# q for dK in an attention backward kernel: from a copy by tokens in DRAM to replicated copies on GpSimd and DMA transposes on chip

## The chip, the cores and the metric

The kernel runs on one core of a Trainium2 chip. The metric is the device time of one execution in microseconds (us). PE is TensorE, DVE VectorE, ACT ScalarE, POOL GpSimd, SP SyncE; SP does no arithmetic here and issues DMAs. POOL issues DMAs too, between its own operations. Each engine works through its instructions in program order.

## What is computed

The output and all gradients of two attention blocks whose outputs stand side by side. Block A is linear attention. Block B, which the change concerns, has 16 query heads and one shared key and value head (S = 2048 tokens, D = 448, head size 28). In short:

```python
q = (x @ wq).reshape(B, S, H, Dh).transpose(0, 2, 1, 3)
k = x @ wk
v = x @ wv
scores = einsum("bhqd,bkd->bhqk", q, k) * Dh ** -0.5
p = softmax(scores)
o = einsum("bhqk,bkd->bhqd", p, v)
b = o.transpose(0, 2, 1, 3).reshape(B, S, H * Dh) @ wo
out, vjp = jax.vjp(...); grads = vjp(grad_out)
```

The gradient of k is dK = sum over heads and queries of dS (keys by queries) times q. For it q must lie with the queries on the partitions, in the order that the transposed dS has.

## The kernel before

Work on block A and the projections of block B fill the first 218 us: `phase_A`, then `phase_B_pre`, which leaves q in SBUF as `R1` (`qT`, `qT_B`): per group g of four heads a tile of 128 partitions (four heads of 32 rows: a shift row, 28 rows of q, padding) by 2048 tokens.

Then comes the core loop (line 894), its order written out by hand under `tc.manual_schedule()`: the instructions of each engine run in the order in which the lines stand. It has `NU + 28` = 540 iterations u. The scores are cut into 64 blocks b of 8 iterations: a block is a chunk `qc` of 256 queries (8 of them) and a pair of heads (8 of them), an iteration is two key tiles of 128. What belongs to a block is spread over later iterations by fixed lags (`due(u, lag)`):

- iteration u computes scores on PE and their exp on ACT in two halves (lines 914 and 964, tile `eT`), and for iteration w = u-16 the product dS: its first half on DVE (line 925), its second by a copy on ACT (`cp`, line 927) and a product on POOL (line 928, tile `dsT`);
- DVE transposes dS in 32x32 blocks into `dsx` two iterations later (line 995);
- every fourth iteration (u%4 = 3) SP issues a DMA transpose of four iterations' `eT` into `eN` (line 966), read by `dv_mm` from u = 8b+20 on (line 978);
- the block's end takes POOL too: `o_norm` at u = 8b+10 makes `prod`, `don` and a copy (lines 808, 811, 812); `row_D` at u = 8b+12 reduces `prod` on DVE and finishes `don` on POOL (lines 816, 817); `don_T` on PE at u = 8b+14 transposes `don` (line 825), and the dS of block b needs the result from u = 8b+16 on;
- `dk_m` (line 834) multiplies `dsx` by `qX`, from u = 8b+27 on, two iterations at a time.

`qX[qc]` is q of one chunk with the queries on the partitions. The transposed dS has 32 queries in each of four partition groups a (for four groups of keys), so q stands there four times: `qX[qc]` is [128, 4, 2, 512], partition 32a+j holding tokens (b, j, s) of the chunk for every a. Before, it is made through DRAM:

- `phase_B_pre` transposes the first 1024 tokens by four DMA transposes into `qn` (line 598) and stores them in `qn_d` in DRAM (line 599), both on SP;
- the entry of the loop transposes the other 1024 into SBUF on SP (line 893), and POOL stores them at u = 34, 42, 50, 58 (line 930);
- four DMAs on POOL per chunk load 256 KB each from `qn_d`, one per partition group a (line 937): for chunk 0 at u = 10 to 22, chunk 1 at u = 66 to 78, and chunk qc from 2 on at u%64 = 34, 42, 50, 58 of the chunk before.

`qX` alternates between two pools of one buffer each. `wo` (line 940) is the output weight, loaded by POOL from DRAM at u = 86. `put_shift` (line 617) writes the shift rows of q by four small DMAs on POOL per 512 tokens; for the second half of the tokens it stands at u = 1.

## Time and profile before

| | |
|---|---|
| median of three runs | 1078.32 us (1070.82 to 1080.0) |
| the profiled execution | 1082.27 us, span of its instructions 1080.6 us |
| start of core loop (first exp) | 218.5 us |
| granted TensorE clock | 0.994 |
| busy: PE, DVE, ACT, POOL | 1026, 898, 873, 774 us |
| DMA packets of the queue of SP | 174 MB of 199 MB moved |
| qX loads (line 937) | 32 on POOL, issue 577 ns each, landing 3.5 to 13.2 us after issue |

The profile is one execution. Busy time is the time in which an engine had an instruction running. The chain follows the work that ended last back to what released it. A group's line has the engine and operation, tiles written and read, shapes, count, busy time and mean duration, then the idle time before it and what ended that idle time. Times in timelines are from the start of the span.

### The profile page before, as it was taken

To read this page: it belongs to the slowest core of one execution; us is meant where nothing else is said; L and a number is where in the kernel's file an instruction comes from. 1 tells how busy PE (TensorE), PEld (TensorE's weight loads), DVE (VectorE), ACT (ScalarE), POOL (GpSimd) and SP (SyncE) were. 2 spreads that over 40 slices of the span, in tenths; PEclk is the share of its full clock that TensorE was granted. 3 is DMA by queue.
4 is the path that set the end of the run, shared out by engine and by line. 5 is a ranking of instruction groups with operands and counts; after the bars stand their busy time and mean duration, and the time that the engine had idled before them with its cause. 6 is when DMAs were issued, how large, how long until landed. Compare 5 with 4: busy or idle time off the path is not lost.

```text
span 1080.6 us, 39970 instructions
## 1 busy us (share of the span) xinstructions
PE 1026.0 (95%) x16241; PEld 484.7 (45%) x16241; DVE 898.0 (83%) x1793; ACT 873.2 (81%) x1741; POOL 774.0 (72%) x1018
## 2 busy tenths in 40 slices
PE   9999999996999999999999999999999999999998
PEld 5555545432444444444444444444444444444434
DVE  7887400556999999999999999999999999999933
ACT  6463122585999999999999999999999999999622
POOL 6001242235899888888988988988988898888881
PEclk9999999997999999999999999999999999999999
DMA  9759899199999999999999999999999999999973
GB/s 265 160 110 199 173 204 228 30 185 151 204 208 211 203 202 188 200 180 210 179 185 197 196 195 187 203 181 188 185 209 187 196 198 162 206 187 181 223 133 90
DMA packets 668305, 199.34 MB, mean 184 GB/s; under 512 B 646056, under 2 KB 663760, under 8 KB 668120
## 3 DMA queue, kind: packets, MB, share of 16 engines
q1 hardware_dynamic: 655256, 174.18, 95.7%
q0 software_dynamic: 7904, 18.64, 6.8%
q10 hardware_dynamic: 4960, 3.96, 1.3%
q8 instruction: 127, 2.08, 0.8%
q14 instruction: 58, 0.48, 0.1%
HBM read 20.99 MB, written 12.94 MB: 31 GB/s over the span
## 4 chain that ended last, share of the span: by engine, by line
PE 37%; POOL 21%; ACT 18%; DVE 11%; issue 10%; DMA 4%; ACTq 0%; DVEq 0%; POOLq 0%
POOL dsT L928 16%; PE agen L82 14%; ACT cp L927 9%; ACT eT L964 7%; PE agen L661 7%; PE aacc L82 7%; PE aacc L661 6%; DVE dsx L995 4%; DVE dsT L925 2%; DMA eN<-eT 2%; POOL prod L808 2%; POOL don L811 1%; POOL R L812 1%; ACT eT L914 1%; DMA qX<-qn_d 1%
## 5 line engine op out<-in xcount | busy, mean ns | idle before, releaser
L928 POOL TENSOR_TENSOR dsT<-cp,eT 128x512 bf16<-128x512 bf16 x512 | 587.8, 1156 | 103.7 <-ACT cp L927 97.2
L995 DVE STREAM_TRANSPOSE dsx<-dsT 128x512 f32<-128x512 f32 x512 | 358.0, 699 | 2.8 <-POOL dsT L928 0.3
L925 DVE TENSOR_TENSOR dsT<-agen,eT 128x512 bf16<-128x512 f32 x512 | 342.1, 668 | 20.0 <-PE agen L661 15.2
L661 PEld LDWEIGHTS <-R 32*128 32x128 bf16 (+1 forms) x9104 | 225.3, 94 | 276.1 <-issue 239.5
L914 ACT ACTIVATE eT<-aacc 128x512 bf16<-128x512 f32 x512 | 313.2, 612 | 26.7 <-PE agen L661 15.8
L927 ACT ACTIVATE cp<-agen 128x512 bf16<-128x512 f32 x512 | 315.4, 616 | 12.3 <-PE agen L661 11.2
L964 ACT ACTIVATE eT<-aacc 128x512 bf16<-128x512 f32 x512 | 321.7, 628 | 0.0
L661 PE MATMUL agen<-dsx,qX 32*32 32x512 bf16 x4096 | 269.0, 376 | 3.5 <-DMA qX<-qn_d 3.5
L661 PE MATMUL agen<-doT,R 32*128 32x256 bf16 x2048 | 248.1, 270 | 3.3 <-DVE dsT L925 1.6
L661 PE MATMUL aacc<-R,R 32*128 32x256 bf16 (+1 forms) x2240 | 218.8, 269 | 5.8 <-DVE oTs L804 1.3
L661 PE MATMUL agen<-eT,R 128*32 128x256 bf16 x2048 | 158.2, 275 | 0.1
L661 PE MATMUL agen<-dsT,R 128*32 128x256 bf16 x2048 | 157.3, 275 | 0.1
L661 PEld LDWEIGHTS <-qX 32*32 32x32 bf16 x4096 | 80.1, 89 | 118.4 <-issue 54.6
L661 PE MATMUL aacc<-eN,don 128*32 128x512 bf16 x1024 | 98.1, 383 | 4.3 <-DMA eN<-eT 4.3
L82 PEld LDWEIGHTS <-R 128*128 128x128 bf16 (+1 forms) x517 | 41.0, 99 | 43.9 <-issue 12.3
L407 POOL COPY pk<-R 128x256 bf16<-128x256 bf16 x4 | 1.6, 397 | 73.8 <-DVE R L367 73.7
L82 PE MATMUL agen<-R,R 128*128 128x448 bf16 (+1 forms) x180 | 42.9, 366 | 0.5 <-ACT R L226 0.5
L661 PEld LDWEIGHTS <-don 128*32 128x32 bf16 x1024 | 33.9, 98 | 5.3 <-issue 4.7
L423 DVE TENSOR_TENSOR osb<-aacc,pr 64x448 bf16<-64x448 f32 x2 | 1.2, 617 | 39.1 <-DMA out_dram<-osb 24.9
L825 PE MATMUL aacc<-identB,don 128*32 128x128 bf16 x256 | 18.6, 224 | 14.0 <-POOL don L817 10.2
L949 DVE TENSOR_SCALAR R<-agen 64x256 bf16<-64x256 f32 x64 | 27.3, 427 | 3.6 <-PE agen L661 1.6
L517 ACT ACTIVATE wdq<-agen 128x448 bf16<-128x448 f32 x16 | 8.7, 543 | 24.7 <-PE agen L82 24.7
(232 smaller groups left out, 987.7 us busy)
## 6 DMA issues: line engine op xcount, KB each, us to landing
qX<-qn_d POOLq DMA_DIRECT2D x32, 256.0 KB, 4.4
out_dram<-osb ACTq DMA_DIRECT2D x22, 112.0 KB
eN<-eT SPq DMA_TRANSPOSE x128
xa<-in_A_x_dram SPq DMA_DIRECT2D x8, 224.0 KB
ga<-in_grad_out_dram SPq DMA_DIRECT2D x4, 448.0 KB
xa<-in_grad_out_dram POOLq DMA_DIRECT2D x4, 448.0 KB, 5.8
out_dram<-wdq POOLq DMA_DIRECT2D x8, 224.0 KB, 4.9
eT<-in_grad_out_dram SPq DMA_DIRECT2D x4, 448.0 KB
```

Of the source, the lines that this page charges most:

```text
L82: nc.tensor.matmul(out_ap, lhsT=lhsT, rhs=rhs, start=start, stop=stop, tile_position=(0, 0))
L661: nc.tensor.matmul(out, lhsT=lhsT, rhs=rhs, start=start, stop=stop, tile_position=pos, skip_group_check=True)
L808: nc.gpsimd.tensor_tensor(out=prod[b][:], in0=dnv, in1=os_, op=ALU.mult)
L811: nc.gpsimd.tensor_tensor(out=dn[:], in0=dnv, in1=r_[:].to_broadcast([P, 2, 2, 32]), op=ALU.mult)
L825: nc.tensor.transpose(tp2[q:q + 32, qb * P:(qb + 1) * P], don[b][:, qb, h, :], identB[:, :], tile_position=(0, q))
L914: nc.scalar.activation(out=eT(u)[:, 0, :], in_=sp[0][:, :], func=ACT.Exp, scale=scale)
L925: nc.vector.tensor_tensor(out=dst[:, 0, :], in0=dp[0][:, :], in1=ew[:, 0, :], op=ALU.mult)
L927: nc.scalar.activation(out=cp[:, :], in_=dp[1][:, :], func=ACT.Copy)
L928: nc.gpsimd.tensor_tensor(out=dst[:, 1, :], in0=cp[:, :], in1=ew[:, 1, :], op=ALU.mult)
L949: nc.vector.tensor_scalar(out=qT_B[g][64 * hp:64 * hp + 64, qc * 256:(qc + 1) * 256], in0=oq[64:128, 0:256], scalar1=scale, scalar2=None, ...
L964: nc.scalar.activation(out=eT(u)[:, 1, :], in_=sp[1][:, :], func=ACT.Exp, scale=scale)
L995: nc.vector.transpose(out=dsx[b][:, tp, :, :, :].rearrange("p h t c -> p (h t c)").bitcast(F32), in_=dsT[y][:, :, :].rearrange("p h c -> p ...
```

## The change

`qn`, `qn_d` and all that reads or writes them go. In the loop, POOL copies q of one chunk and one group of four heads from `R1` into a new tile `qst` (one buffer), four times side by side, in two instructions (one for each s) in two successive iterations; then SP issues one DMA transpose of `qst` (128x1024) into the columns of group g of `qX[qc]`. For chunk 0 this happens at u = 0 to 7, two iterations per group, the transpose in the second; for chunk qc+1 at u%64 = 32 to 63 of chunk qc, eight iterations per group: copies at u%8 = 0 and 1, after that iteration's product on POOL, the transpose at u%8 = 3, on SP behind that iteration's transpose of `eT`. The load of `wo` moves from u = 86 to the entry of the loop. `qX[0]` and the even chunks move to the other of the two pools.

```diff
-            if qc == 1:
-                for g in range(4):
-                    nc.sync.dma_start_transpose(qn[:, :, g * P:(g + 1) * P], qT[:, g, 0:1024])
-                nc.sync.dma_start(qn_d[0:1024, :].rearrange("(t p) c -> p t c", p=P), qn)
...
+        qst = pp_.tile([P, 8, 4, 32], BF16, name="qst", bufs=1)
...
+        def qc_copy(qc, g, s):
+            src = qT_B[g][:, qc * 256:(qc + 1) * 256].rearrange("p (b j s) -> p b j s", b=4, s=2)[:, :, :, s]
+            nc.gpsimd.tensor_copy(out=qst[:, :, :, :].rearrange("p (b s) a j -> p b s a j", s=2)[:, :, s, :, :],
+                                  in_=src.unsqueeze(2).to_broadcast([P, 4, 4, 32]))
...
-            qn = pqa_.tile([P, 8, 512], BF16, name="qX")
-            for g in range(4):
-                nc.sync.dma_start_transpose(qn[:, :, g * P:(g + 1) * P], R1[:, g, 1024:2048])
+            nc.gpsimd.dma_start(wo, wo_d[:, 0:D].rearrange("(g p) c -> p g c", p=P))
+            qc_T = None
...
-                for n in {34: (0,), 42: (1,), 50: (2,), 58: (3,)}.get(u, ()):
-                    nc.gpsimd.dma_start(qn_d[1024 + 256 * n:1280 + 256 * n, :].rearrange("(t p) c -> p t c", p=P),
-                                        qn[:, 2 * n:2 * n + 2, :])
-                for a in {10: (0,), 14: (2,), 18: (1,), 22: (3,), 66: (0,), 70: (2,), 74: (1,), 78: (3,)}.get(u, ()) or {
-                        34: (0,), 42: (2,), 50: (1,), 58: (3,)}.get(u % 64, ()) * (96 < u < 448):
-                    qc = u // 64 + (u > 96)
-                    if a == 0:
-                        qX[qc] = (pqa_ if qc % 2 else pqb_).tile([P, 4, 2, 512], BF16, name="qX")
-                    nc.gpsimd.dma_start(qX[qc][32 * a:32 * a + 32, :, :, :].rearrange("j b s c -> j b (s c)"),
-                                        qn_d[qc * 256:(qc + 1) * 256, :].rearrange("(b j s) c -> j b (s c)", b=4, s=2))
-                if u == 86:
-                    nc.gpsimd.dma_start(wo, wo_d[:, 0:D].rearrange("(g p) c -> p g c", p=P))
+                if u < 8 or 32 <= u % 64 and u < 448:
+                    qc, (g, i) = (0, divmod(u, 2)) if u < 8 else (u // 64 + 1, divmod(u % 64 - 32, 8))
+                    if i == 0 and g == 0:
+                        qX[qc] = (pqb_ if qc % 2 else pqa_).tile([P, 4, 2, 512], BF16, name="qX")
+                    if i < 2:
+                        qc_copy(qc, g, i)
+                    if i == (1 if u < 8 else 3):
+                        qc_T = (qc, g)
...
+                    if qc_T:
+                        qc, g = qc_T
+                        nc.sync.dma_start_transpose(
+                            qX[qc].rearrange("p b s c -> p (b s) c")[:, :, g * P:(g + 1) * P], qst[:, :, :, :].rearrange("p n a j -> p (n a j)"))
+                        qc_T = None
```

The last lines stand behind the transpose of `eT` (line 966) and, like it, under `if hasS`.

## The prediction

> **What bounds the kernel now.** I read the page first (parts 1, 4, 5), then the chain in order of time and the waits for the first 60 us of the core loop, then the timeline of POOL for one group of eight iterations, then the DMA transposes on SP by tile, source line and timeline.

> ```profile
> PE 1026.0 (95%) x16241; PEld 484.7 (45%) x16241; DVE 898.0 (83%) x1793; ACT 873.2 (81%) x1741; POOL 774.0 (72%) x1018
> POOL dsT L928 16%; PE agen L82 14%; ACT cp L927 9%; ACT eT L964 7%; PE agen L661 7%; PE aacc L82 7%; PE aacc L661 6%; DVE dsx L995 4%; DVE dsT L925 2%; DMA eN<-eT 2%; POOL prod L808 2%; POOL don L811 1%; POOL R L812 1%; ACT eT L914 1%; DMA qX<-qn_d 1%
> L928 POOL TENSOR_TENSOR dsT<-cp,eT 128x512 bf16<-128x512 bf16 x512 | 587.8, 1156 | 103.7 <-ACT cp L927 97.2
> L407 POOL COPY pk<-R 128x256 bf16<-128x256 bf16 x4 | 1.6, 397 | 73.8 <-DVE R L367 73.7
> ```

> The core loop is 540 iterations u. The start times of L914 in the trace put u=0 at 218.5 us and u=511 at 1003.6 us, about 1.5 us each. In the stretch 500 to 600 us ACT is busy 99%, DVE 98%, PE 96%, POOL 89%: no engine has room, and POOL's L928 is the longest entry of the chain although POOL idles 104 us before it.

> Start of the loop, chain in order of time and waits:

> ```profile
> 232.62 16.89 DMA eN<-eT
> 255.79 10.60 DMA qX<-qn_d
> ```

> ```profile
> PE aacc L661 <- DMA eN<-eT: 4.3, 1, 4.3
> PEld L661 <- DMA qX<-qn_d: 3.8, 1, 3.8
> ```

> Two transfers are late there: the second eN transpose, then the fourth qX load. Iterations 16 to 23 take 19.1 us and 24 to 31 take 18.8 us, where 40 to 63 take 12.3 us per eight.

> Steady state, POOL's timeline (start, duration; last column the idle time before):

> ```profile
> 595.23 1.15 POOL L928 TENSOR_TENSOR dsT<-cp,eT 128x512 bf16<-128x512 bf16 x1 [0.32 <-ACT cp L927]
> 596.33 0.57 POOL L937 DMA_DIRECT2D qX<-qn_d  x1
> 596.91 0.44 POOL L808 TENSOR_TENSOR prod<-R,oTs 128x128 f32<-128x128 bf16 x1
> 597.30 0.41 POOL L811 TENSOR_TENSOR don<-R,rl 128x128 bf16<-128x128 bf16 x1
> 597.77 0.29 POOL L812 CAST R<-oTs 128x128 bf16<-128x128 f32 x1
> 598.02 2.26 POOL L928 TENSOR_TENSOR dsT<-cp,eT 128x512 bf16<-128x512 bf16 x2
> 600.25 0.21 POOL L817 TENSOR_TENSOR don<-Dq,rl 128x4 bf16<-128x4 f32 x1
> ```

> At u%8=2 POOL falls 1.3 us behind and has caught up by u%8=7. With a qX load in the group, eight iterations take 12.16 us; without, 12.0. The 0.15 us sits at u%8=6, where PE waits for don (L817). So POOL has no slack left in a group with a load: whatever it loses at u%8=0 to 4 comes out again as a wait of PE at u%8=6.

> SP, by tile, source line and timeline (durations ns min/median/max in the first two):

> ```profile
> L966 SPq DMA_TRANSPOSE eN<-eT x128: 4760/5421/12268, 226.6 to 1005.2; - x128
> ```

> ```profile
> L598 SPq DMA_TRANSPOSE gaT<-R x4: 1243/1269/1386, 212.4 to 216.7; - x4
> ```

> ```profile
> 1011.01 1.28 SPq L955 DMA_TRANSPOSE R<-R  x1
> ```

> An eN transpose holds SP 5.25 us from the end of its exp in a group without a load, 5.8 us with one, out of 6.05 us per four iterations. L598 and this L955 have the new transpose's size (128x1024). By the semaphore updates in the trace, L598 landed 3.4 us after it began, on idle DMA engines; the L955, issued behind an eN, 4.7 us after.

> [...] while qX loads run, eN goes from 5.25 to 5.8 us, and to 9 and 12 us at 232 and 241 us. [...] The trace has 2.0 to 3.4 us from the end of a 128x1024 transpose on SP to its last update. [...] here all are on SP, so the new ones queue with eN. [...] copies of 256 and 448 elements take 397 and 561 ns, 0.85 ns each.

> **The change, step by step**, against the profiled execution's span of 1080.6 us (1082.3 us by its own clock; the median of the runs shown is 1078.3, so I carry differences over to that).

> Removed. (a) The congestion at the start: 19.1+18.8 us for u=16 to 31. From the undisturbed even and odd iterations around them (1.45 odd, 1.8 even while do_proj runs, 1.5 later) I make it 13.0+12.3, so -12.5. (b) The last qX load (u=442) landed 13.2 us after issue; its eN held SP 8.5 us and the group took 13.5 us, not 12.15: -1.4. (c) The loads of u=66 to 78: 12.17, 12.15 against 12.0: -0.3. The four stores L930 and nine transposes and one store on SP before the loop (212 to 227 us) go too; u=0 does not wait for them, since PE's sel matmuls end at 217.9 and its first score matmuls follow at once. Their worth is in (a).

> Copies for loads in steady state. Two copies of 512 elements: 0.185+512x0.00085=0.62 us each, about 0.58 back to back, against one load issue of 0.58 in the same group. Copies stand at u%8=0 and 1. POOL's lag in a group, from L928 at 1.13 back to back and iterations of 1.48, 1.45, 1.68, 1.45: +0.25, +0.55, then the three of L808 to L812 to 1.2 at u%8=3 (now 1.27), and L817 starts with 0.88 (now 0.91). Net 0. Bounds for the copy, whose source steps two elements and repeats four times: 0.55 to 0.8 us, as no copy here has that pattern; each 0.1 us costs 0.2 per group, so -2 to +11 over 28 groups. I take 0.

> The new wait. qst is one buffer. Copies of group g+1 (u%8=0) wait until the transpose of group g has landed, and that one is issued at u%8=3 behind the eN of the same iteration. From the end of that exp: eN 5.25, gap 0.1, new transpose 1.3, landing 2 to 3.4 later, I take 2.9 (between L598's 2.0 and the L955's 3.4): 9.5 us. POOL reaches the copy when L928 of u%8=0 ends, 8.26 us after the same exp (mean of the second halves). So POOL stands about 1.25 us. Behind the copy on POOL are L928, L808 to L812, L817; for these wait the DVE transposes (L995), row_D and don_T, so PE loses it at u%8=6. That slip moves the next copy too, so the next group waits little: of four groups the first copy is free, the second and fourth wait. 2x1.2x7=17 us. Bounds: landing 2.0 gives about 5, 3.9 gives 27. SP itself: 5.25+1.4+5.25+0.2=12.1 per group of 12.16, just enough.

> The start. POOL now: wo load issue to 219.0, first copy to 220, put_shift (8x0.56) to 224.5; the second copy waits for these to land (they share POOL's queue with wo's 448 KB), about 226.2. Transpose 0 is issued at 226.9 and lands at 230.3; copies 1 to 231.5; transpose 1 stands behind eN(3) (228.1 to 233.2), lands 237.8; copies 2 to 239, transpose 2 lands 242.5; copies 3 to 243.7. Only then L808 of block 0, which ran at 233.6. DVE waits in row_D(0), PE in don_T(0): +9.8, with PE idle. eN and qX are then in time (eN(7) lands about 248.5, needed about 252.7). Bounds: 5 to 13. Moving wo costs its 0.8 us there, counted.

> Sum: -12.5-1.4-0.3+9.8+17=+12.6, a span of 1093 and a run of **1091 us**. Own range of this case 1084 to 1099.

> **Rivals.** (1) The landing is early enough (8.3 us or less after the exp): POOL doesn't stand, the start gives +9.8 against -14.2: -4, 1074 (to 1078 with small waits). For it: SP lands some small transposes 1.1 us after their end early in the trace. Against: those were alone. Chance 0.22. (2) The other side, faster: the round trips at the start don't hold POOL. If copies 3 are done before L808 of block 0 is due (233.6), all -14.2 stays; with early landings as in (1), 1064. It decides from 4 us per round trip less than I have; eN(3) in between speaks against it. Chance 0.08. (3) Landing at 3.9 us or copies at 0.8 us: +24 to +32 in all, 1102 to 1110. Both in part give the same. Chance 0.18. The transposes might also make dv_mm late: its slack is 13 iterations (19 us) against about 9; left out.

> **How the numbers follow.** Main case 0.52. The bound of 1% (about what can be told from no change) is 1067.5 and 1089.1. Faster: rival 2, 0.08. Within: rival 1 and the lower third of the main case, 0.39. Slower: the rest, 0.53. The range 1070 to 1112 leaves out rival 2 and the far end of 3.

> **What would show it.** In the new profile: waits of POOL's qst copy on DMA qX<-qst, about 1.2 us each and some 14 to 21 of them in the loop; a chain with DMA qX<-qst in it; at the start one long wait of PE or DVE for POOL prod or don near 235 to 245 us and no wait for eN; PE's waits at L825 for POOL don grown from the 32 us of now; copies near 0.6 us; eN back to about 5.3 us everywhere. If the copies wait for nothing, my landing time is wrong; if PE still waits for eN or qX, the start is.

## The result, and the profile after

The changed kernel takes **1110.99 us** (median of four runs, 1110.52 to 1113.82), against 1079.16 us for the kernel before beside it: ratio 1.0318, 95% interval 1.0264 to 1.0373. The forecast was 1091 us. The measured time has the forecast's sign and lies inside its range, but the loss, 32 us, is two and a half times the 12.6 us of the sum. The profiled execution ran 1110.71 us with a span of 1109.0 us; the granted TensorE clock is 0.98, where it was 0.994.

The page of the changed kernel, parts 1, 2, 4 and 5 (PEld is TensorE's weight load; a group's line: busy us and mean ns, then the idle time before it):

```profile
PE 1038.0 (94%) x16241; PEld 488.2 (44%) x16241; DVE 898.7 (81%) x1793; ACT 874.3 (79%) x1741; POOL 788.0 (71%) x1046
...
PEclk9999999988999999999999999999999999999999
...
POOL dsT L928 16%; PE agen L81 14%; ACT cp L927 11%; ACT eT L960 8%; PE agen L656 8%; PE aacc L656 7%; PE aacc L81 6%; DMA qX<-qst 2%; POOL qst L832 2%; DVE dsx L996 2%; DVE dsT L925 1%; ACT eT L914 1%; PE aacc L821 1%; POOL prod L804 1%; POOL don L807 1%
...
L928 POOL TENSOR_TENSOR dsT<-cp,eT 128x512 bf16<-128x512 bf16 x512 | 588.3, 1156 | 92.5 <-ACT cp L927 86.0
...
L832 POOL COPY qst<-R 128x512 bf16<-128x512 bf16 x64 | 38.9, 611 | 35.8 <-DMA qX<-qst 29.1
```

DVE and ACT do the work they did, to about 1 us, and no share says what was lost. What is new is a group that stands before it works: the 64 copies are busy 38.9 us and POOL is idle 35.8 us ahead of them, 29.1 us of that for the landing of a transpose. PE is busy 12 us *longer* for the same 16241 matmuls: they ran slower. Who waits, over the whole span (total us, times, longest):

```profile
PEld L821 <- POOL don L813: 40.3, 44, 10.9
...
POOL qst L832 <- DMA qX<-qst: 29.1, 16, 5.1
...
PE aacc L821 <- POOL don L813: 26.3, 16, 10.6
...
DVE Dq L812 <- POOL prod L804: 16.9, 10, 11.7
```

PE now waits 66.6 us for `don` in `don_T` (L821); before (there L825) it was 32.0 us:

```profile
PEld L825 <- POOL don L817: 21.8, 45, 1.5
...
PE aacc L825 <- POOL don L817: 10.2, 29, 1.2
```

By the start times of L914, u=511 begins 29.3 us later than before. 1.5 us of that is the entry of the loop, 220.0 against 218.5 us; the kernels below enter at 218.0 to 220.2 us whatever is changed in them, so this isn't the change's. (Each of the seven traces that enter at 220.0 us or later has 3.4 us at a granted clock of 0.50 at 51 us, and none of the other seven has.) The first 32 iterations take 59.1 us (57.3 before). In the windows of 64 iterations the second halves, u%64 = 32 to 63, of the first seven, where the copies stand, take 26.5 us more; all the rest of the loop takes 0.6 us less.

One such stand, that is, a time in which POOL has work and waits, on the timeline of POOL (start, duration; in brackets the idle time before):

```profile
596.71 0.61 POOL L832 COPY qst<-R 128x512 bf16<-128x512 bf16 x1 [1.32 <-DMA qX<-qst]
597.26 0.58 POOL L729 DMA_DIRECT2D out_dram<-R  x1
597.87 1.17 POOL L928 TENSOR_TENSOR dsT<-cp,eT 128x512 bf16<-128x512 bf16 x1
...
603.96 0.21 POOL L813 TENSOR_TENSOR don<-Dq,rl 128x4 bf16<-128x4 f32 x1
```

The copy of u%8=0 waits 1.32 us. Seven microseconds on, `don` is finished that much later (L813), and PE, which has stood in `don_T` for it, goes on. What that does to PE shows in the same stretch cut into four windows of 3.4 us (window, its length, then busy us and count by engine, PEclk, DMA share, GB/s):

```profile
597.60:601.00 3.40, 3.22 (x64) 1.37 (x64) 2.63 (x5) 3.16 (x7) 3.38 (x5) 1.00 1.16 207
601.00:604.40 3.40, 1.72 (x34) 0.59 (x30) 2.77 (x5) 2.91 (x6) 3.34 (x7) 1.00 1.17 113
604.40:607.80 3.40, 3.40 (x48) 1.13 (x38) 2.32 (x4) 1.61 (x4) 2.29 (x3) 0.50 1.49 277
607.80:611.20 3.40, 3.16 (x76) 1.46 (x72) 2.75 (x6) 2.89 (x7) 2.47 (x3) 0.99 0.92 133
```

In the second window PE is busy half the time. In the third the granted clock is 0.50 ("half clock" below), and PE, busy without a pause, gets through 48 matmuls where the window behind it has 76. The group of eight iterations takes 15.35 us in place of 12.0: 1.3 us of standing, half a microsecond for the store of an output tile that POOL issues in this group (L729), and 1.5 us of slow clock. The stand was in the prediction; the clock was not.

### The profile page after: what moved, and what is told of

Its sections match the earlier page's. It is cut to its first block, busy times and chain, and to the rows that moved or that the text cites. A ratio compares the mean times of both kernels' runs of the same rounds, so it can differ in the third digit from the quotient of the medians.

```text
span 1109.0 us, 40031 instructions
## 1 busy us (share of the span) xinstructions
PE 1038.0 (94%) x16241; PEld 488.2 (44%) x16241; DVE 898.7 (81%) x1793; ACT 874.3 (79%) x1741; POOL 788.0 (71%) x1046
## 4 chain that ended last, share of the span: by engine, by line
PE 38%; POOL 21%; ACT 21%; issue 11%; DVE 5%; DMA 3%; ACTq 0%; SPq 0%; POOLq 0%; DVEq 0%
POOL dsT L928 16%; PE agen L81 14%; ACT cp L927 11%; ACT eT L960 8%; PE agen L656 8%; PE aacc L656 7%; PE aacc L81 6%; DMA qX<-qst 2%; POOL qst L832 2%; DVE dsx L996 2%; DVE dsT L925 1%; ACT eT L914 1%; PE aacc L821 1%; POOL prod L804 1%; POOL don L807 1%
## 5 line engine op out<-in xcount | busy, mean ns | idle before, releaser
L928 POOL TENSOR_TENSOR dsT<-cp,eT 128x512 bf16<-128x512 bf16 x512 | 588.3, 1156 | 92.5 <-ACT cp L927 86.0
L925 DVE TENSOR_TENSOR dsT<-agen,eT 128x512 bf16<-128x512 f32 x512 | 342.0, 668 | 19.7 <-PE agen L656 14.7
L914 ACT ACTIVATE eT<-aacc 128x512 bf16<-128x512 f32 x512 | 312.9, 611 | 53.2 <-PE agen L656 26.2
L927 ACT ACTIVATE cp<-agen 128x512 bf16<-128x512 f32 x512 | 314.7, 615 | 12.3 <-PE agen L656 11.2
L656 PE MATMUL agen<-dsx,qX 32*32 32x512 bf16 x4096 | 272.5, 381 | 0.0
L656 PE MATMUL aacc<-R,R 32*128 32x256 bf16 (+1 forms) x2240 | 222.9, 271 | 6.5 <-DVE oTs L800 1.1
L656 PE MATMUL agen<-eT,R 128*32 128x256 bf16 x2048 | 160.5, 278 | 0.1
L832 POOL COPY qst<-R 128x512 bf16<-128x512 bf16 x64 | 38.9, 611 | 35.8 <-DMA qX<-qst 29.1
L81 PEld LDWEIGHTS <-R 128*128 128x128 bf16 (+1 forms) x517 | 41.2, 99 | 44.6 <-issue 13.3
L821 PE MATMUL aacc<-identB,don 128*32 128x128 bf16 x256 | 18.8, 225 | 33.6 <-POOL don L813 26.3
L656 PEld LDWEIGHTS <-don 128*32 128x32 bf16 x1024 | 34.5, 98 | 0.6
L821 PEld LDWEIGHTS <-don 128*32 128x32 bf16 x256 | 11.0, 94 | 47.9 <-POOL don L813 40.3
```

The source lines that it names most:

```text
L81: nc.tensor.matmul(out_ap, lhsT=lhsT, rhs=rhs, start=start, stop=stop, tile_position=(0, 0))
L656: nc.tensor.matmul(out, lhsT=lhsT, rhs=rhs, start=start, stop=stop, tile_position=pos, skip_group_check=True)
L821: nc.tensor.transpose(tp2[q:q + 32, qb * P:(qb + 1) * P], don[b][:, qb, h, :], identB[:, :], tile_position=(0, q))
L832: nc.gpsimd.tensor_copy(out=qst[:, :, :, :].rearrange("p (b s) a j -> p b s a j", s=2)[:, :, s, :, :], in_=src.unsqueeze(2).to_broadcast([ ...
L914: nc.scalar.activation(out=eT(u)[:, 0, :], in_=sp[0][:, :], func=ACT.Exp, scale=scale)
L925: nc.vector.tensor_tensor(out=dst[:, 0, :], in0=dp[0][:, :], in1=ew[:, 0, :], op=ALU.mult)
```

## Experiments

**Theory.** The loop loses by the meeting of the copy at u%8=0 with the landing of a transpose that was queued behind eN on SP. Each stand of POOL costs its own length, and in seven of the 14 cases a stretch of half clock on PE besides. **Rivals:** the copies' time on POOL; the 32 more transposes on SP and the DMA engines, making eN late; at the start, DMA traffic in place of the chain on POOL.

**1. The transpose at u%8=2.** One digit of the changed kernel is changed:

```diff
-                    if i == (1 if u < 8 else 3):
+                    if i == (1 if u < 8 else 2):
```

> The loop's q transposes are issued at u%8=2 instead of 3, so they stand in SyncE's order with no eN transpose directly ahead of them; one staging tile, copies and number of DMAs as in the changed kernel. Theory (the copy of the next group waits for the landing of a transpose that was queued behind eN, and each such stand of GpSimd idles TensorE): the transpose lands about 4 us after u%8=2, long before u%8=0, GpSimd's wait on it in the loop falls from about 25 us to under 2, each second half of a window comes back to 97-98 us per 64 iterations, time 1111 - 26 = 1085 (1081-1089). Rival (the 64 DMAs more on the same queue and DMA engines make eN or other loads late): no change, 1107-1112. Rival (the GpSimd time of the copies itself): no change, 1107-1112.

Measured: **1079.69 us**, ratio to the kernel before 0.9998 (0.9969 to 1.0027). The second halves take 48.0 to 48.6 us where they took 50.7 to 54.5, 30.1 us less in all. Waits in the loop, 262 to 1000 us, of which none is for qst:

```profile
PEld L821 <- POOL don L813: 16.7, 42, 1.1
PE aacc L821 <- POOL don L813: 4.9, 14, 0.8
```

The same copies, the same 32 transposes (64 is the number of the copies), one buffer: both rivals for the loop fall. The 30.1 us are above the 26 expected because copies in place of loads turned out better than even, see below; the start, which was not changed, was 3.4 us shorter in this execution besides (see "The start").

**2. The copies alone**, in the kernel before, where nothing reads what they write:

```diff
+                if 32 <= u % 64 and u < 448 and u % 8 < 2:
+                    qc_copy(u // 64 + 1, (u % 64 - 32) // 8, u % 8)
```

> The kernel before with the loop's 56 copies added on GpSimd at their places; nothing reads the tile they write, and q still comes by DRAM. Theory (waits, not work): GpSimd has the time, 1079 within 4 us. Rival (the 0.6 us copies delay GpSimd's dsT products, and TensorE with them): the second halves grow by 3 to 4 us each, 1100-1106.

Measured: **1092.57 us**, 1.0104 (1.008 to 1.0128), between the two ranges expected. Groups take 12.55 us where the kernel before has 12.16 and experiment 1 has 12.0: a load issue (0.58 us) in a group costs 0.15 us, two copies (1.2 us) cost nothing, all three 0.55 us. So the two copies use up what POOL can take ahead of `don`; the changed kernel stands right at that limit. That fits with every stand of POOL coming out whole at PE.

**3. The start alone.** Chunk 0's copies go into four tiles of the dsT pool:

```diff
+                    if u < 8 and i == 0:
+                        qstart[g] = pd_.tile([P, 2, 512], BF16, name="dsT").rearrange(
+                            "p h (n a j) -> p (h n) a j", a=4, j=32)
```

> Chunk 0 alone: its four copies go into four tiles that are free then (of the dsT pool), so no copy at u<8 waits for a transpose; the loop keeps its one tile and its late transposes. Theory (the start loses its gain to the chain copy-transpose-copy on GpSimd, which makes prod and don of block 0 late at u=14): u 0-31 falls from 59.1 us to 48-50 us, time 1111 - 10 = 1101 (1098-1104). Rival (the first blocks are slow for another reason, DMA traffic of the output weight and the q rows at entry): u 0-31 stays at 57-60, time 1108-1112.

Measured: **1104.04 us**, 1.0216 (1.0161 to 1.0272). u=0 to 31 takes 49.15 us, not 59.13; u=14 takes 1.16 us, not 12.20. The start is as the theory says. The total gives back 7 us and not 10, just outside the range expected: from u=32 to 511 this execution took 2.9 us more than that of the changed kernel.

**4. Both edits**, those of 1 and 3.

> Both edits: transposes at u%8=2 and own tiles for chunk 0. Theory: the two add, 1111 - 26 - 10 = 1075 (1070-1080), a little faster than the kernel before. Rivals as with each alone: 1085 if the start has another cause, 1101 if the loop has.

Measured: **1070.85 us**, 0.991 (0.9878 to 0.9941). They add. At u=20 there was a new stop; waits between 240 and 256 us:

```profile
DVE dsT L930 <- DMA qX<-dsT: 2.6, 1, 2.6
```

The dsT product of u=20 got the tile that the fourth transpose of chunk 0 was still reading: borrowed storage, the same kind of wait at another place. So the copies of chunk 0 moved into a `dsx` buffer, which is needed from u=26 on:

```diff
+        stage0 = px_.tile([P, 8, 2, 2, 256], BF16, name="dsx").rearrange(
+            "p (g n) h t c -> p g (n h t c)", g=4)[:, :, 0:1024].rearrange("p g (n a j) -> p g n a j", a=4, j=32)
```

> Transposes at u%8=2, and chunk 0's four copies into four parts of a dsx buffer (first needed at u=26) instead of dsT tiles (needed again from u=16). Theory (in the earlier form VectorE's dsT product of u=20 waited for a transpose that still read its tile): the stop at u=20 and its slow iterations go, u 0-31 falls from 50.1 to 45-46 us, time 1071 - 4.5 = 1066 (1062-1070). Rival (u=20 stands for something else): 1069-1073.

Measured: **1069.66 us**, 0.9897 (0.9854 to 0.9939). u=0 to 31 takes 45.80 us, with no stop. The total lies in both ranges expected; it is the stop that went which decides. Of the 4.3 us gained there, the profiled execution gave 3.0 back in one group at u=56 to 63, where a copy still waited 1.64 us for a transpose and half clock followed. That transpose belongs to u=50, and SP began it at u=55:

```profile
300.05 1.26 SPq L972 DMA_TRANSPOSE qX<-qst  x1
```

It landed 3.5 us after its end, within the 1.3 to 3.9 us of the others; what was late is SP. With the transposes of chunk 0 in its queue it falls 10 us behind at the start, and in the first window its eN still begin 4 to 7 us after their exp. The q transposes of that window start 6.1 to 7.1 us after the exp of their iteration, those of the other windows 0.4 to 4.8 us. So even at u%8=2 there is little room while SP is behind.

**5. A stand without a DMA.** In that kernel, idle copies of growing size on POOL stand in for the wait:

```diff
+                    if qc and i == 0 and g % 2:
+                        qf = qst[:, :, :, :].rearrange("p n a j -> p (n a j)")
+                        for n in [1024] * (qc // 4) + [256 * (qc % 4)] * (qc % 4 > 0):
+                            nc.gpsimd.tensor_copy(out=qf[:, 0:n], in_=R1[:, 0, 0:n])
```

> A GpSimd copy that does no work for the result is put ahead of the q copies at u%64=40 and 56, of 256, 512, 768, 1024, 1280, 1536 and 1792 elements in windows 1 to 7 (about 0.3 to 2.1 us); transposes at u%8=2 and own tiles for chunk 0, so GpSimd never waits for a transpose in the loop. It stands in for the wait. Theory (TensorE is idle as long as GpSimd is late[...]): groups of eight iterations take 12.0 us plus the copy up to about 1.1-1.2 us, and from 1.3 us on 12.0 plus the copy plus 1.5 to 2 us, with 2 to 3 us of granted clock near 0.6 behind don_T. Rival (the low clock has to do with the transposes or the DMA wait, not with the idle): 12.0 plus the copy at every size, clock 1.0.

Measured in one execution: **1091.62 us**. Without an idle copy the two groups take 12.55 (12.0 in windows 1 and 2) and 12.0 us; the first also issues the store of an output tile on POOL. A star marks a group with a stretch of half clock:

```
window                 1      2      3      4      5      6      7
idle copy, us       0.40   0.61   0.82   1.04   1.44   1.64   1.87
group of u%64=40   13.79  12.67  14.62* 15.04* 14.12  16.20* 14.54
group of u%64=56   12.44  12.67  12.88  13.09  14.86* 13.76  15.40*
```

(13.79 holds a real wait of 1.3 us for a transpose as well; it is the only one of this loop.) Without a star a group takes its base plus the copy, to 0.13 us; with one, 1.25 to 1.53 us more, and 2.0 us in column 6, where the half clock lasted two windows of the raster below. So the half clock needs no DMA wait, and the rival falls. But the step that I expected, between 1.2 and 1.3 us, is wrong too: 0.82 us brought a stretch and 1.64 us did not. In the traces of the kernels before and changed every change of the clock lies on one raster of 3.413 us (the stretches of half clock from 232 to 990 us are 3.413, 6.827 and 17.067 us long), so I took PE's busy share in the raster window just ahead (busy with the profile's modelled ends). In these two traces, from 232 to 990 us, ten windows at full clock were busy 0.26 to 0.61, and half clock followed all ten; the other 418 were busy 0.64 or more, and it followed none. Counted over these and the twelve traces of this study, of windows busy under 0.54, 21 of 21 were followed by half clock; from 0.54 to 0.64, 11 of 20; above 0.64 none. In idle time, up to 1.2 of the 3.41 us never brought half clock in these traces and 1.6 us or more always did. In them the longest gap does not tell: windows with one gap of 1.19 us went both ways (changed kernel at 628.3 us, busy 0.50, half clock; at 904.8 us, busy 0.65, none). In column 6 of the table, the stand of u%64=40 fell into one window, 780.7 to 784.1 us:

```profile
777.30:780.70 3.40, 3.38 (x62) 1.37 (x59) 2.73 (x6) 3.33 (x7) 3.38 (x5) 1.00 1.26 230
780.70:784.10 3.40, 1.98 (x30) 0.63 (x29) 2.47 (x5) 2.34 (x6) 3.33 (x6) 0.99 1.19 174
784.10:787.50 3.40, 2.71 (x40) 1.25 (x44) 2.10 (x5) 1.46 (x4) 2.85 (x4) 0.50 1.17 217
787.50:790.90 3.40, 3.40 (x64) 1.25 (x54) 2.34 (x5) 2.61 (x6) 1.48 (x2) 0.50 0.63 117
```

The last line shows why the count is of windows at full clock: PE was busy for 0.80 of the window before it, and the half clock stayed. What ends a stretch is not worked out here.

**6. The stands left, PE kept busy.** The changed kernel with eight matmuls, read by nothing, ahead of `don_T` in the groups that stand; and the same eight in experiment 1:

```diff
+                if u % 16 == 14 and u % 64 > 32 and 32 < u < 448:
+                    for _ in range(8):
+                        mm(spare[:, 128:512], identB[:, :], kT_rep[:, 0:384], start=True, stop=True)
```

> The changed kernel, its waits left as they are, with eight matmuls of 128x128 by 384 columns, read by nothing, ahead of don_T at u%64=46 and 62, where TensorE stands (about 1.3 us of work in 14 groups). Theory (the second half of each stall's price is the clock after an idle TensorE): TensorE's idle stretch is short, the clock stays at 1.0, groups with a stall of over 1.2 us take 13.3-13.9 us instead of 15.2, time 1111 - 15 = 1096 (1090-1101). Rival (the low clock comes from the load itself or at random, so more matmuls only add): 1111 + 5 to + 18.

> Control: the same eight matmuls in the kernel with the transposes at u%8=2, where TensorE hardly waits. They cost their own time less the wait that they fill: 0.5 to 1.2 us in 14 groups, 1080 + 7 to + 17 = 1087-1097. Both theories agree here; it shows what the fillers cost by themselves.

Measured: **1103.9 us**, 1.0214 (1.0172 to 1.0255), and **1097.4 us**, 1.0154 (1.0106 to 1.0202). More work made the changed kernel 7 us faster, and the other 18 us slower. Of the 7 us the fillers account for 5.3, in the second halves of the profiled executions; 3.5 us lie in u=0 to 31, before the first filler (see "The start"), and the rest of the loop took 1.0 us more. The waits, 300 to 940 us, first of the changed kernel, then of the one with fillers:

```profile
POOL qst L832 <- DMA qX<-qst: 17.3, 13, 2.2
PE aacc L821 <- POOL don L813: 15.7, 15, 1.2
```

```profile
POOL qst L832 <- DMA qX<-qst: 17.4, 13, 2.1
...
PE aacc L821 <- POOL don L813: 2.1, 3, 1.2
```

POOL stands just as long, but PE does not idle, and from 262 us on the clock never falls (seven stretches in the changed kernel). In the 14 groups the price of a stand is 14.26-12.20=2.06 us without fillers (changed kernel against experiment 1) and 13.81-13.33=0.48 us with them. The 5.3 us are a third of the 15 us expected, since the fillers themselves take 1.3 us where a stand is shorter than that.

**7. The copies moved in place of the transposes:** in the loop at u%8=2 and 3, the transpose behind eN at u%8=3 as in the change.

```diff
+                v = u if u < 8 else u - 2
+                if u < 8 or 8 <= v and 32 <= v % 64 and v < 448:
+                    qc, (g, i) = (0, divmod(v, 2)) if u < 8 else (v // 64 + 1, divmod(v % 64 - 32, 8))
...
+                    if i == 1:
```

> The changed kernel with nothing but GpSimd's loop copies moved from u%8=0 and 1 to 2 and 3; the transposes stay behind eN at u%8=3, one staging tile, start as changed. Theory (it is the meeting of the copy at u%8=0 with a landing 9.7 us after the exponential of u%8=3): GpSimd comes to the copy at u%8=2 some 11 us after that exponential, so it waits in none or one of the groups; second halves 48-49 us each, time as with the transposes at u%8=2, 1080 (1076-1086). Rival (the transposes behind eN hurt by themselves, by a late eN): 1105-1112.

Measured: **1095.32 us**, 1.0126 (1.0024 to 1.0228); both numbers missed. POOL waits for no transpose in the loop, as the theory says, with SP's order untouched; and no stretch of half clock follows. But all 28 groups take 12.69 us. Waits, 300 to 940 us:

```profile
PEld L821 <- POOL don L813: 31.4, 37, 1.2
PE aacc L821 <- POOL don L813: 21.8, 26, 0.9
```

At u%8=2 the copies stand ahead of `prod` and `don`, whose last reader is due at u%8=6; at 0 and 1 POOL has two iterations more to catch up before it comes to the last of those. I read this from the order of POOL's instructions; experiments 8 and 10, with the copies behind `don`, agree with it. I had counted the wait and not the place.

**8. The copies behind don:** at u%8=5 and 6, each transpose at the next u%8=0, chunk 0 in the dsx buffer.

```diff
+                v = u if u < 8 else u - 5
...
                     if i == (1 if u < 8 else 3):
```

> Own tiles for chunk 0 in a dsx buffer; the loop's copies at u%8=5 and 6 and each transpose at the next u%8=0, where no eN and no store of an output tile stands with them. Theory (with the transposes at u%8=2 the second group of each window still took 12.55 us, where an output tile's store is issued on GpSimd beside the copies, u%64=40): all groups 12.0 us, 5 x 0.55 = 3 us off 1069.7: 1066 (1063-1070). Rival (copies ahead of don's last write at u%8=4 or of o_norm at u%8=2 matter more, or another cause): 1068-1075.

Measured: **1073.26 us**, 0.9957 (0.9936 to 0.9979), a miss. All groups without a stop take 12.0 us, that of u%64=40 too, as expected. But POOL waited 12 times for a transpose, the longest time 4.6 us:

```profile
POOL qst L838 <- DMA qX<-qst: 15.3, 12, 4.6
```

I had placed the transposes at u%8=0, and SP is then in the eN of u%8=7 for 5.3 us, so they start only as that ends and land about as the next copy comes. The longest wait is in the first window, where the eN of SP still begin 5 us late. It is the error of the change once more.

**9. The output weight's load** back at u=86, in the kernel of experiment 4 with the dsx buffer:

```diff
-            nc.gpsimd.dma_start(wo, wo_d[:, 0:D].rearrange("(g p) c -> p g c", p=P))
...
+                if u == 86:
+                    nc.gpsimd.dma_start(wo, wo_d[:, 0:D].rearrange("(g p) c -> p g c", p=P))
```

> Transposes at u%8=2 and own tiles in a dsx buffer, with the output weight's load back at u=86. Theory (the load at entry moves 448 KB in about 4.3 us where the queues have room, and costs nothing; at u=86 likewise): 1069.7 within 3. Rival (the load at entry delays the first transposes and blocks): u 0-31 falls below 45.8 us and the time to 1066 or less. Other rival (at u=86 it makes eN late): over 1072.

Measured: **1068.55 us**, 0.9881 (0.9796 to 0.9967), the same as with the load at entry. (From issue to landing the load took 4.0 us at entry in the trace of the changed kernel, and 4.9 us at u=86 in that of before.) That part of the change costs and brings nothing that can be seen.

**10. All together.** The kernel of experiment 4 with the dsx buffer, with copies at u%8=5 and 6 and the transpose at 6, where SP comes to it as the eN of u%8=3 ends:

```diff
-                if u < 8 or 32 <= u % 64 and u < 448:
-                    qc, (g, i) = (0, divmod(u, 2)) if u < 8 else (u // 64 + 1, divmod(u % 64 - 32, 8))
+                v = u if u < 8 else u - 5
+                if u < 8 or 8 <= v and 32 <= v % 64 and v < 448:
+                    qc, (g, i) = (0, divmod(v, 2)) if u < 8 else (v // 64 + 1, divmod(v % 64 - 32, 8))
...
-                    if i == (1 if u < 8 else 2):
+                    if i == 1:
```

> Own tiles for chunk 0 in a dsx buffer; the loop's copies at u%8=5 and 6 (behind don's last write at u%8=4, far from o_norm at u%8=2), each transpose at u%8=6. SyncE is held 5.3 us by each eN (u%8=3 and 7), so it comes to the q transpose at about u%8=6.6 and the landing, some 4 us later, is at u%8=1 to 2 of the next eight, three iterations ahead of the next copy. Theory: GpSimd never waits for a transpose in the loop, all groups 12.0 us, 1064 (1060-1068), 1.5% under the kernel before. Rival (the q transpose now delays the eN of u%8=7, and the matmuls that read it, by 1 us and more): second halves over 49 us, 1070-1080.

Measured: **1065.15 us**, 0.9871 (0.9832 to 0.9911), inside the range expected and the fastest here, 46 us under the changed kernel. Its page:

```profile
PE 1021.3 (96%) x16232; PEld 489.4 (46%) x16241; DVE 895.4 (84%) x1793; ACT 870.4 (82%) x1741; POOL 788.7 (74%) x1046
...
PEclk9999999999999999999999999999999999999999
...
L838 POOL COPY qst<-R 128x512 bf16<-128x512 bf16 x56 | 34.1, 609 | 0.5 <-DMA qX<-qst 0.5
```

The same 64 copies (eight now write the dsx buffer) and POOL as busy as in the changed kernel, and the wait ahead of them is 0.5 us in place of 29.1. It falls in the first window, where SP begins the q transposes 6.3 to 8.4 us after the exp of their iteration; later it is 1.5 to 6.2 us. No stretch of half clock is left from 225 to 1000 us.

## Why the prediction was wrong in size

**Removed, (a) the congestion at the start, -12.5.** An undisturbed u=0 to 31 takes 45.80 us (experiment 4), against 57.27 in the trace of before: -11.5. Right to 1 us; but in experiment 2 the same start took 50.8 us, so this loss of the kernel before varies from one execution to the next. **(b), (c), the other loads, -1.7,** and **copies for loads, net 0:** the copies take 0.61 us as expected, groups without a stand take 12.0 us, not 12.16. Second halves without a stand or a store beside the copies take 48.0 us, where the trace of before has 48.6 and once 50.0. Over seven windows that is -6.7 with (b), so this part was better than I had it. Two readings were off without changing a sum: the load of u=442 landed 10.7 us after issue (the 13.2 us belong to one at u=18), and the transposes before the loop are eight, not nine.

**The start, +9.8.** The chain of round trips is there. The chain of waits of the changed kernel (start, us, what):

```profile
237.19 3.16 DMA qX<-qst
240.47 1.18 POOL qst L832 x2
241.67 3.21 DMA qX<-qst
...
245.56 0.61 POOL qst L832
246.17 0.39 POOL prod L804
246.57 0.35 POOL don L807
```

`prod` of block 0 starts at 246.2 us; I had 243.7, with an entry 1.5 us earlier. u=14 lost 11.0 us. Not in the sum: 17 us of half clock, which cost 2.4 us in u=15 to 17.

One wait of the chain differs from execution to execution, that of the second copy for the shift rows (`put_shift`); I had it end at 226.2 us, with the entry at 218.5. First the changed kernel (entry at 220.0), then experiment 1 (218.5):

```profile
230.23 0.61 POOL L832 COPY qst<-R 128x512 bf16<-128x512 bf16 x1 [3.41 <-DMA R<-R]
...
226.69 0.61 POOL L832 COPY qst<-R 128x512 bf16<-128x512 bf16 x1 [1.43 <-DMA R<-R]
```

Five kernels of this study have this start. In the two whose trace has the long wait (the changed kernel and the second of experiment 6), u=0 to 31 takes 58.9 to 59.1 us with 17 us of half clock; in the three with the short one (experiments 1, 7 and the first of 6), 55.6 to 55.7 us with 10 us. So up to 3.5 us between two of these executions come from the start and not from what was edited. Why the rows land later in some executions is open.

**The new wait, 2x1.2x7=17: this is the step that failed.** Its mechanism holds line by line: POOL free 8.19 us after the exp (8.26 forecast), landing 9.6 us after it in the mean, 8.7 to 11.2 (9.5), second and fourth group of each four. The gaps ahead of the copies of u%8=0 sum to 20.5 us (17.3 us of it in the 13 waits that the profile puts to a transpose in 300 to 940 us, so 1.3 each for my 1.2). But "PE loses it" was taken as PE losing just that. Seven of the 14 groups take 15.05 to 15.45 us: 22.7 us over 12.0, for 11.9 us of standing and 1.7 us of output stores in three of them. The other 9.1 us are seven stretches of half clock, one behind each. Experiments 5 and 6 show that it is PE's idleness that brings them. Nor does my upper bound of 27 follow from my own sum: a landing at 3.9 us makes 10.55-8.26=2.3 us a stand, 32 us for fourteen. The seven second halves lie 33 us above 48.0 each, but not by such landings: 20.5 of it are stands, 9.1 half clock, 2.8 the stores beside copies in five groups.

**The sum** against the two spans: expected +12.6, measured +28.4. The stands gave 3.5 more, the half clock in the loop 9.1, the stores 2.8, the start 4.6 (1.0 less gain, 1.2 longer chain, 2.4 clock) and the entry 1.5; the loads gave back 5.6 more and the tail 0.8. That makes 15.1 of the 15.8.

**Rivals.** (1) and (2), early landings and a start without a hold, didn't come. (3) comes nearest with its 1102 to 1110, but has not the cause: neither the copies (0.61 us) nor the mean landing (9.6 us) was off. What was to show it came nearly all: waits of qst on DMA qX<-qst 16 times (13 of them in 300 to 940 us, 1.3 us each), DMA qX<-qst in the chain, one wait of 11.7 us of DVE for prod, PE's waits in `don_T` grown from 32.0 to 66.6 us, eN at 5.22 us, no wait of PE for eN or qX worth naming.

## What to carry to other kernels

A staging tile with one buffer ties its writer to the landing of the transfer behind it (16 waits, 29.1 us, in the changed kernel); before choosing where the transfer is issued, look at what holds the issuing queue at that point (here eN, 5.3 of every 6 us), and let it start as that ends, with iterations to spare before the next write. Price a stand of an engine that TensorE waits for not at its length alone: in the changed kernel's loop seven stands left TensorE busy for 0.50 to 0.61 of one 3.413 us window of the clock's raster, and each brought some 1.3 us more (9.1 us for the seven). And look where a new operation stands in its engine's order against the next operation with a deadline: the same two copies cost nothing at u%8=0 and 0.69 us per group at u%8=2.
